# Another order for the steps of a planned attention-plus-MLP kernel

## The chip, the cores and the metric

The kernel runs on one core of one Trainium2 chip. The metric is the device time of one execution in microseconds, the median of several runs. Before the change it is 181.74 us (three runs, 180.81 to 182.94). The core's engines are PE (matmul), DVE (vector), ACT (scalar, activation), POOL (GpSimd) and SP, which issues nearly all of this kernel's DMAs from one queue. Each takes its instructions strictly in the order of its own list; semaphores tie the lists together.

## The reference

The first part is a linear attention with a decaying state, for batch 4, 8 heads, 768 steps and head size 48. Per head and step t:

```
cur   = (u * k_t) outer v_t
y_t   = r_t @ (state + cur)
state = w_t * state + k_t outer v_t
```

The second part is an MLP over the 3072 tokens (y with its heads laid side by side, 384 wide):

```
h = x @ w_in          # 384 -> 2048
g = max(0.01 * h, h)
out = g @ w_out       # 2048 -> 384
```

Inputs and output are float32.

## The kernel before, in words

**Tiling.** The sequence is cut into 24 chunks (named c0 to c23 here) of 128 steps, six for each of the four batches. The first two chunks of two batches are done as two *pairs* (c0 with c1, c2 with c3; the function `pair`), the other 20 one by one (`single`), some with their score matmuls merged. For a chunk, four DMAs load w, k, r and v (192 KB each) into one of ten `in` buffers. ACT takes the logarithm of w (L778, "Ln"), PE sums it over the steps with a triangular matrix (the *cum* step, L784 and L787), DVE makes an inclusive sum `ci` (L796), ACT takes exponents (L805, L810, L814), DVE multiplies them into r and k (L468), PE or a DMA transposes these (L479, L831), PE makes the scores (L925), DVE masks them (L855), and PE multiplies them with v (*intra*, L896) and the carried state with r (L891). PE also forms the chunk's contribution to the state (*sums*, L865, and L650 for a pair). POOL casts v to bf16 (`vb`, L518), scales the carried state (`sb`, L842), and makes the `u` term (*bonus*: L498 and L502 multiply, DVE reduces at L506, L510 gives `vs`). DVE adds the bonus (L541), and the output is transposed into `xT` (*typose*, L527, then a copy at L532 or L534, or a DMA at L910).

**The MLP** runs in 15 blocks (0 to 14) of one or two chunks. The *up* steps (L1087) multiply `xT` with `w_in`, ACT applies the leaky relu (L1102) into `g`, the *down* steps (L1117, four per chunk) multiply with `w_out`, ACT or DVE copies the result into one of five `o` buffers (L1128, L1130), and SP stores it (L1134). The last three blocks save matmuls with a seven-product scheme (`seven`: products L1019, sums L1002, combinations L1033, L1035, L1040, stores L1070). The weights are loaded in float32 at the start and cast to bf16 piece by piece on DVE, ACT or POOL (L411, L413, L415).

**What sets the order.** Every step above is added to a `Plan` as an entry with the engines that may do it and an assumed duration on each, a priority number, the steps it depends on, and the buffers it reads and takes. There are 1090 steps. Before any instruction is issued, `Plan.order` walks through assumed time: whenever an engine is free, it takes from the ready steps the one with the lowest priority number, if the buffers are there. The outcome is one list of steps per engine, and the steps are then issued in that order. Two tables are applied just before: `RANK` adds a number to the priority of single steps, and `FORCE` pins a step to one engine.

```
        for i, x in RANK.items():
            plan.steps[i][2] = round(plan.steps[i][2] + x, 3)
        for i, e in FORCE.items():
            plan.steps[i][0] = {e: plan.steps[i][0][e]}
        order = plan.order(pools)
```

In the first 24 us of assumed time, gaps on PE are filled with matmuls on zeros (L1159), as many as fit the assumed gap.

A *place* below is the position of a step in the list of its engine, from 0; an *entry* of SP is the same for its DMAs.

Of the kernel before, what the change touches and what calls it, by code (L numbers as in the profile page):

```python
# [23 lines left out]
class Plan:  # L24
# [135 lines left out]
STORE = (0.45, 8, 0.9, 0.2)  # L160
TRK = (1.7, 64, 0.9, -0.6)
TY = (0.95, 24, 0.7, -0.6)
RANK = {0: 15.37, 1: 14.4, 2: 3.33, 3: 23.03, 5: 38.76, 6: 12.01, 7: -26.8, 8: -21.87, 9: -21.96, 10: -19.05,
# [63 lines left out]
FORCE = {24: "DVE", 27: "DVE", 30: "ACT", 31: "DVE", 47: "ACT", 59: "ACT", 62: "ACT", 80: "ACT", 86: "DVE",  # L227
    113: "DVE", 115: "ACT", 118: "DVE", 120: "ACT", 122: "ACT", 124: "DVE", 126: "POOL", 128: "ACT", 129:
    "POOL", 135: "POOL", 138: "DVE", 140: "POOL", 143: "ACT", 144: "POOL", 493: "DVE", 501: "ACT", 605: "DVE",
    613: "ACT", 905: "DVE", 911: "DVE", 933: "ACT", 953: "ACT", 967: "ACT", 1003: "ACT", 1031: "ACT", 1076:  # L230
    "ACT", 1081: "ACT"}


@with_exitstack
def kernel(
# [95 lines left out]
    with tc.manual_schedule():  # L331
# [810 lines left out]
        step({"PE": 0.0}, lambda e: None, 1000.0, deps=[up_first[2]], reads=[warm])  # L1142
# [51 lines left out]
```

## Time and profile before

| | |
|---|---|
| median of three runs | 181.74 us (180.81 to 182.94) |
| the profiled execution, its own time | 180.97 us |
| its span, first to last instruction | 179.3 us |
| mean granted PE clock | 0.997 |
| PE busy | 170.3 us, 95% of the span |
| weight loads on PE | 133.8 us, 75% |
| DVE, ACT, POOL busy | 131.9, 116.5, 103.4 us |
| DMA: all transfers | 34.43 MB, mean 192 GB/s |
| `in` loads of a single chunk | 192 KB each, 4.2 us from issue to landing (median) |

Busy times are unions of an engine's instructions and are averages over stages with different limits: the first 24 us (loading, first pairs, weight casts), a long middle in which chunks and MLP blocks interleave, and the last 10 us, in which only the MLP's last products are left. Where an engine's row shows a wait, it names what ended last before the instruction could start. "issue" in the chain of waits is time in which nothing that the profile shows was waited for.

### The profile page before, as it was taken

The page shows a single profiled execution, that of the slowest core. Times are in us where ns is not written, and L with a number is a line of the kernel's source. Part 1 is how long each engine was busy: PE and PEld are TensorE (multiplying, and loading weights), DVE is VectorE, ACT ScalarE, POOL GpSimd, SP SyncE. Part 2 cuts the span into 40 slices and gives each one's busy share as a digit, 9 for nine tenths or more (in the row PEclk, how much of TensorE's full clock was granted, in tenths as well). Part 3 has the DMA queues.
Part 4 walks back from the last instruction along what each step waited for, and adds up shares of the span by engine and source line. Part 5 has one row for each costly group of instructions (what it writes and reads, how often), then busy time and mean ns, then how long its engine had stood idle before and what let it go on. Part 6 is the DMA issues. An engine that isn't in the chain of part 4 may idle for free.

```text
span 179.3 us, 5364 instructions
## 1 busy us (share of the span) xinstructions
PE 170.3 (95%) x2102; PEld 133.8 (75%) x2105; DVE 131.9 (74%) x266; ACT 116.5 (65%) x259; POOL 103.4 (58%) x138
## 2 busy tenths in 40 slices
PE   7798899999989999999999999999999999999991
PEld 2555778867868688787688777777778798899991
DVE  7799664189769899459687659499787599777472
ACT  4679868855957688895379775176685487735620
POOL 5998532675697586878468855414996448110000
PEclk9999999999999999999999999999999999999998
DMA  6999999999999899999999999979799996813004
GB/s 150 261 284 317 371 378 358 185 195 201 227 185 203 170 223 143 182 208 184 200 199 194 220 178 229 208 151 140 146 205 140 195 214 139 184 24 115 0 22 154
DMA packets 116716, 34.43 MB, mean 192 GB/s; under 512 B 109138, under 2 KB 115923, under 8 KB 116691
## 3 DMA queue, kind: packets, MB, share of 16 engines
q1 hardware_dynamic: 116688, 34.09, 94.6%
q8 instruction: 16, 0.26, 0.7%
q14 instruction: 10, 0.07, 0.2%
q10 hardware_dynamic: 2, 0.00, 0.0%
HBM read 25.17 MB, written 4.72 MB: 167 GB/s over the span
## 4 chain that ended last, share of the span: by engine, by line
PE 57%; DMA 12%; POOL 8%; issue 7%; SPq 6%; DVE 4%; ACT 4%; DVEq 0%; POOLq 0%; ACTq 0%
PE ps L1087 26%; PE ps L1117 14%; DMA in<-in_v_dram 8%; PE ps L1019 6%; SPq L553 4%; DMA in<-in_k_dram 3%; PE ps L925 2%; POOL ru L498 2%; SPq L389 2%; DMA in<-in_r_dram 2%; ACT g L1102 2%; POOL ru L502 2%; POOL sb L842 1%; DVE o L1040 1%; PE ps L896 1%
## 5 line engine op out<-in xcount | busy, mean ns | idle before, releaser
L1087 PE MATMUL ps<-xT,w_in_b 128*128 128x256 bf16 (+1 forms) x720 | 73.2, 251 | 0.2 <-ACT xT L534 0.2
L1102 ACT ACTIVATE g<-ps 128x512 bf16<-128x512 f32 x96 | 56.5, 595 | 20.7 <-PE ps L1087 15.2
L1087 PEld LDWEIGHTS <-w_in_b 128*128 128x128 bf16 x720 | 57.5, 98 | 9.2 <-issue 0.7
L1117 PE MATMUL ps<-w_out_b,g 128*128 128x384 bf16 x288 | 56.0, 326 | 0.1
L1117 PEld LDWEIGHTS <-g 128*128 128x128 bf16 x288 | 25.7, 97 | 12.3 <-ACT g L1102 0.2
L498 POOL TENSOR_TENSOR ru<-in,ub 128x384 f32<-128x384 f32 x24 | 24.6, 1028 | 11.0 <-DMA in<-in_k_dram 10.8
L468 DVE TENSOR_TENSOR rk<-in,ps 128x384 bf16<-128x384 f32 x48 | 25.0, 549 | 7.4 <-ACT ps L810 4.2
L855 DVE TENSOR_TENSOR m<-ps,maskb 128x512 bf16<-128x512 f32 x40 | 25.4, 684 | 6.1 <-PE ps L925 5.1
L502 POOL TENSOR_TENSOR ru<-ru,in 128x384 f32<-128x384 f32 x24 | 24.3, 1018 | 2.7 <-DMA in<-in_r_dram 2.1
L842 POOL TENSOR_TENSOR sb<-s,a 128x384 bf16<-128x384 f32 x18 | 15.7, 873 | 8.9 <-ACT a L805 8.7
L510 POOL TENSOR_TENSOR vs<-in,dg 128x384 f32<-128x384 f32 x20 | 16.6, 828 | 7.4 <-DVE dg L506 4.9
L518 POOL CAST vb<-in 128x384 bf16<-128x384 f32 x24 | 12.0, 504 | 12.0 <-DMA in<-in_v_dram 12.0
L506 DVE TENSOR_REDUCE dg<-ru 128x8 f32<-128x384 f32 x24 | 13.1, 546 | 2.3 <-POOL ru L502 2.1
L796 DVE TENSOR_TENSOR ci<-ps,lw 128x384 f32<-128x384 f32 x20 | 11.1, 554 | 3.7 <-PE ps L784 1.7
L778 ACT ACTIVATE lw<-in 128x384 bf16<-128x384 f32 x20 | 10.4, 520 | 3.0 <-DMA in<-in_w_dram 3.0
L810 ACT ACTIVATE ps<-ps 128x384 f32<-128x384 f32 x20 | 9.5, 474 | 4.1 <-DVE ci L796 3.8
L541 DVE TENSOR_TENSOR y<-ps,vs 128x384 bf16<-128x384 f32 x20 | 11.1, 554 | 1.4 <-PE ps L896 0.6
L880 DVE TENSOR_TENSOR s<-ps,sb 128x384 f32<-128x384 f32 x14 | 7.7, 552 | 3.9 <-PE ps L865 1.4
L814 ACT ACTIVATE ps<-ci 128x384 f32<-128x384 f32 x20 | 9.8, 488 | 0.6 <-DVE ci L796 0.6
L805 ACT ACTIVATE a<-ps 64x4 f32<-64x4 f32 x36 | 6.0, 167 | 5.6 <-DVE ci L796 3.8
L534 ACT COPY xT<-ps 128x384 bf16<-128x384 bf16 x11 | 5.2, 478 | 6.9 <-PE ps L527 6.9
L1019 PEld LDWEIGHTS <-g 128*128 128x128 bf16 x96 | 8.0, 98 | 0.5 <-ACT g L1102 0.4
(105 smaller groups left out, 222.3 us busy)
## 6 DMA issues: line engine op xcount, KB each, us to landing
out_dram<-o SPq DMA_DIRECT2D x23, 192.0 KB, 3.2
in<-in_w_dram SPq DMA_DIRECT2D x20, 192.0 KB, 4.2
in<-in_k_dram SPq DMA_DIRECT2D x20, 192.0 KB, 4.2
in<-in_r_dram SPq DMA_DIRECT2D x20, 192.0 KB, 4.3
in<-in_v_dram SPq DMA_DIRECT2D x20, 192.0 KB, 4.3
in<-in_moe_w_out_dram SPq DMA_DIRECT2D x4, 768.0 KB, 12.1
in<-in_moe_w_in_dram SPq DMA_DIRECT2D x4, 384.0 KB, 7.0
in<-in_moe_w_in_dram SPq DMA_DIRECT2D x2, 768.0 KB, 9.2
```

What stands on the lines that cost most here:

```text
L468: (nc.gpsimd if e == "POOL" else nc.vector).tensor_tensor(out=o, in0=x, in1=i, op=ALU.mult)
L498: lambda e: nc.gpsimd.tensor_tensor(out=ru.t[:], in0=kv(), in1=ubv, op=ALU.mult),
L502: lambda e: nc.gpsimd.tensor_tensor(out=ru.t[:], in0=ru.t[:], in1=rv(), op=ALU.mult),
L506: lambda e: nc.vector.tensor_reduce(out=dg.t[:], in_=ru.t[:], axis=AX.X, op=ALU.add),
L510: lambda e: nc.gpsimd.tensor_tensor(out=vs.t[:], in0=vv(), in1=dg.t[:].unsqueeze(2).to_broadcast([128, H, D]), op=ALU.mult),
L518: {"POOL": 0.56}, lambda e: nc.gpsimd.tensor_copy(out=vb.t[:], in_=vv()),
L842: lambda e: nc.gpsimd.tensor_tensor(out=sb.t[:].rearrange("p g a d -> p (g a) d"), in0=s_in.t[:].rearrange("p g a d -> p (g a) d"), in1=a_ ...
L855: lambda e, par=par: nc.vector.tensor_tensor(out=m.t[:, par, :, :], in0=sc[par].t[:].rearrange("p (g t) -> p g t", g=NP), in1=maskb[:].uns ...
L1019: nc.tensor.matmul(o(), lhsT=x()[:, i, :], rhs=y()[:, i, :], start=fresh, stop=(stop and i == ii[-1]), skip_group_check=True)
L1087: nc.tensor.matmul(hp.t[:, a * N : (a + 1) * N], lhsT=w_in_b[:, t, (j + a) * 128 : (j + a + 1) * 128], rhs=xT[:, t, c0 : c0 + N], start=(a ...
L1102: lambda e, hp=hp, g=g, j=j, J=J, N=N: nc.scalar.activation(out=g.t[:, j : j + J, 0:N], in_=hp.t[:, 0 : J * N].rearrange("p (a n) -> p a n ...
L1117: nc.tensor.matmul(op.t[:, 0:DM], lhsT=g.t[:, j, off : off + 128], rhs=w_out_b[:, j, :], start=(j == 0), stop=(j == NJ - 1))
```

## The change

Only the two tables `RANK` and `FORCE` are replaced. No step, no dependency, no buffer count and no assumed duration differs. In the kernel before, `RANK` has entries for steps 0 to 144, 492 to 716 and 902 to 1087, with gaps; in the changed one it has one for every step from 0 to 1087, and nearly all numbers differ. `FORCE` names 36 steps before and 55 after. By the words that come with the change, the numbers were searched with the operations lengthened at random and all results seen a little later than the plan assumes; neither is in the code, which plans with the same durations as before.

```diff
-RANK = {0: 15.37, 1: 14.4, 2: 3.33, 3: 23.03, 5: 38.76, 6: 12.01, 7: -26.8, 8: -21.87, 9: -21.96, 10: -19.05,
...
-    1083: 298.55, 1084: 18.56, 1085: 937.22, 1086: 932.94, 1087: 937.23}
-FORCE = {24: "DVE", 27: "DVE", 30: "ACT", 31: "DVE", 47: "ACT", 59: "ACT", 62: "ACT", 80: "ACT", 86: "DVE",
-    113: "DVE", 115: "ACT", 118: "DVE", 120: "ACT", 122: "ACT", 124: "DVE", 126: "POOL", 128: "ACT", 129:
...
+RANK = {0: 62.8, 1: 61.81, 2: -93.65, 3: -93.65, 4: 52.82, 5: 73.74, 6: -103.67, 7: -194.53, 8: -194.63, 9:
...
+    -18.67, 1083: 478.97, 1084: -18.68, 1085: 975.95, 1086: 975.96, 1087: 975.95}
+FORCE = {6: "DVE", 24: "DVE", 27: "ACT", 30: "ACT", 33: "DVE", 47: "ACT", 57: "ACT", 80: "DVE", 86: "ACT", 89:
+    "DVE", 103: "ACT", 113: "DVE", 115: "DVE", 120: "POOL", 128: "ACT", 129: "DVE", 132: "ACT", 134: "POOL",
...
```

What this does to the lists, counted in the two built programs:

| engine | steps before | steps after | at another place | mean shift, largest |
|---|---|---|---|---|
| PE | 320 | 320 | 245 | 2.7, 23 |
| DVE | 248 | 249 | 189 | 2.0, 19 |
| ACT | 258 | 260 | 198 | 2.6, 20 |
| POOL | 120 | 117 | 100 | 3.1, 11 |
| SP | 144 | 144 | 111 | 3.8, 37 |

41 steps change their engine, most of them copies and casts between DVE and ACT; POOL keeps one weight cast from before, takes two others, and gives five away. The moves that the prediction speaks of:

- SP: the w load of chunk 6 goes from entry 26 to 25, and c6's v load from 31 to 26; c5's v from 25 to 28; c7's k from 33 to 32. The stores of MLP blocks 0 (its first), 1 and 2 go from 27, 34 and 38 to 64, 60 and 65. The w loads of c9, c10 and c11 go from 43, 48 and 53 to 38, 42 and 44.
- PE: the cum steps of c5, c6, c9, c10 and c11 go from 67, 76, 111, 123 and 135 to 63, 72, 109, 121 and 131. The sums of c7 stay at 96. The last eight steps stay.
- POOL: c6's `vs` goes from behind c7's first bonus product to behind c7's cast of v.
- Weight casts: five go to DVE (four from POOL, one from ACT), two leave it (one to ACT, one to POOL); one goes from ACT to POOL and one from POOL to ACT.
- The line numbers of the changed kernel are 73 higher below the tables.

More of the change, by code (lines that the diff above doesn't have):

```diff
@@ L162 @@
 TY = (0.95, 24, 0.7, -0.6)
-RANK = {0: 15.37, 1: 14.4, 2: 3.33, 3: 23.03, 5: 38.76, 6: 12.01, 7: -26.8, 8: -21.87, 9: -21.96, 10: -19.05,
[63 rows of a table removed]
-FORCE = {24: "DVE", 27: "DVE", 30: "ACT", 31: "DVE", 47: "ACT", 59: "ACT", 62: "ACT", 80: "ACT", 86: "DVE",
-    113: "DVE", 115: "ACT", 118: "DVE", 120: "ACT", 122: "ACT", 124: "DVE", 126: "POOL", 128: "ACT", 129:
-    "POOL", 135: "POOL", 138: "DVE", 140: "POOL", 143: "ACT", 144: "POOL", 493: "DVE", 501: "ACT", 605: "DVE",
-    613: "ACT", 905: "DVE", 911: "DVE", 933: "ACT", 953: "ACT", 967: "ACT", 1003: "ACT", 1031: "ACT", 1076:
-    "ACT", 1081: "ACT"}
+RANK = {0: 62.8, 1: 61.81, 2: -93.65, 3: -93.65, 4: 52.82, 5: 73.74, 6: -103.67, 7: -194.53, 8: -194.63, 9:
[134 rows of a table added]
+FORCE = {6: "DVE", 24: "DVE", 27: "ACT", 30: "ACT", 33: "DVE", 47: "ACT", 57: "ACT", 80: "DVE", 86: "ACT", 89:
+    "DVE", 103: "ACT", 113: "DVE", 115: "DVE", 120: "POOL", 128: "ACT", 129: "DVE", 132: "ACT", 134: "POOL",
+    135: "DVE", 137: "ACT", 140: "DVE", 141: "DVE", 144: "POOL", 160: "ACT", 173: "ACT", 189: "ACT", 202:
+    "ACT", 238: "DVE", 262: "ACT", 311: "DVE", 341: "DVE", 343: "ACT", 384: "DVE", 420: "ACT", 422: "ACT",
+    436: "DVE", 501: "ACT", 613: "DVE", 737: "ACT", 743: "ACT", 757: "ACT", 771: "ACT", 785: "ACT", 821:
+    "ACT", 883: "ACT", 905: "ACT", 933: "DVE", 939: "ACT", 953: "ACT", 967: "ACT", 998: "ACT", 1003: "DVE",
+    1031: "ACT", 1076: "ACT", 1081: "ACT"}
 @with_exitstack
```

196 rows, old and new, of the table RANK are left out of this document.

## The prediction

> **What bounds the kernel now.** I read the page from the top first: the share of each engine, and the slices, which tell in which part of the span an engine is full.
>
> ```profile
> span 179.3 us, 5364 instructions
> ...
> PE   7798899999989999999999999999999999999991
> ...
> DMA  6999999999999899999999999979799996813004
> ```
>
> From the sixth slice on (22.4 us) PE is at nine tenths or more in all but the twelfth (49 to 54 us) and the last. DMA is full too, until about 155 us. The view of windows puts numbers to this; its columns are the stretch, its length, then busy time (and instructions) of PE, weight loads, DVE, ACT, POOL, then the granted clock, DMA share and GB/s.
>
> ```profile
> 24.00:48.00 24.00, 24.00 (x288) 18.78 (x286) 14.74 (x28) 17.45 (x36) 13.48 (x16) 1.00 1.12 249
> 48.00:72.00 24.00, 23.20 (x329) 18.77 (x327) 21.32 (x43) 18.15 (x44) 17.18 (x22) 1.00 1.05 189
> 72.00:168.00 96.00, 95.81 (x1106) 76.27 (x1104) 70.16 (x129) 61.67 (x142) 54.22 (x65) 1.00 0.95 170
> ```
>
> From 24 to 168 us PE is idle for 0.80 + 0.19 = 0.99 us of 144. Every matmul of the reference's work is in both kernels, so a new order can win only PE's waits. The view of waits names them; of PE's rows these matter:
>
> ```profile
> PE ps L865 <- POOL vb L518: 0.6, 1, 0.6
> ...
> PE ps L1019 <- DVE o L1040: 0.3, 1, 0.3
> ```
>
> The first is the wait of the twelfth slice, the second lies in the tail; PE's longer ones, in the head (before 24 us), come below. A shown wait is too short by a little, because an end on PE is modelled:
>
> ```profile
> 50.27 1.46 PE L1117 MATMUL ps<-w_out_b,g 128*128 128x384 bf16 x8
> 51.57 0.39 PE L479 MATMUL ps<-ident,rk 128*128 128x128 bf16 x4
> ```
>
> Eight matmuls started at 50.27 and the next form at 51.57, 1.30 us on, while their drawn end (51.73) is 0.16 later. So each wait is about 0.16 longer than shown, and one under 0.16 is not shown at all. Allowing for seven of them after 24 us, the tail's included: 0.99 + 0.3 + 7 x 0.16 = 2.4 us. That is the ceiling of what the order can win behind the head.
>
> **The change part by part.** Counted in the two built programs, of 320 PE steps 245 stand at another place (mean shift 2.7 places, most 23), of 144 SP entries 111 (mean 3.8, most 37); 41 steps go to another engine. Nothing is added but 6 fill matmuls (36 become 42), all in the head.
>
> *Head.* The chain of waits there:
>
> ```profile
> 11.47 8.26 DMA in<-in_v_dram
> ...
> 20.71 0.91 POOL vb L518 x2
> ...
> 21.66 0.47 PE ps L650 x13
> 22.13 0.02 issue
> 22.16 0.57 DVE sb L661
> ...
> 23.69 1.42 PE ps L1087 x12
> ```
>
> The v load of the second pair is entry 10 of SP in both lists (the first is 0), behind the same ten entries. POOL then has four steps for it: bonus, cast, cast, bonus before; cast, bonus, cast, bonus after. The second cast, which PE's state sums (L650) need, is third in both. PE's places 0 to 36 hold the same steps, and places 25 to 45 are the same up to one swap. The first gap-free run of L1087 therefore starts at 23.7 again. The fills added there are short and stand where PE waits anyway (three ahead of the add that needs DVE's sb). Head: 0, with 0.3 us either way as the bound.
>
> *Weight casts.* Five casts come to DVE from POOL and ACT, and two leave it. Their cover:
>
> ```profile
> 33.35 0.56 DVE L413 CAST w_out_b<-in 128x768 bf16<-128x768 f32 x1 [3.68 <-DMA in<-in_moe_w_out_dram]
> ```
>
> DVE is idle for 3.68 us until that weight lands. In the changed list it makes two casts behind that landing, to about 33.35 + 2 x 0.56 = 34.5, and PE's down step that needs them stands at place 58 in both lists, behind c4.cum at 57, which the chain of waits has at 35.36:
>
> ```profile
> 35.36 0.18 PE ps L784
> ```
>
> Cost 0; without that cover, 0.56 each.
>
> *The c6 load.* This is the one place where I find a new wait. PE's list goes there, in before:
>
> ```profile
> 41.13 0.36 PE L896 MATMUL ps<-vb,m 128*128 128x48 bf16 x8
> 41.33 1.46 PE L1117 MATMUL ps<-w_out_b,g 128*128 128x384 bf16 x8
> 42.63 0.33 PE L527 MATMUL ps<-ident,y 128*128 128x128 bf16 x3
> 42.80 0.81 PE L1117 MATMUL ps<-w_out_b,g 128*128 128x384 bf16 x4
> 43.45 0.39 PE L479 MATMUL ps<-ident,rk 128*128 128x128 bf16 x4
> 43.67 0.33 PE L784 MATMUL ps<-lw,trev 128*128 128x384 bf16 x1
> ```
>
> The last is c6.cum. It goes from place 76 to 72: the first row, half of the second, the third and fourth now stand behind it (0.20 + 0.65 + 0.17 + 0.65 = 1.67 us by starts; of the transposes one goes and one comes). PE would be there at 43.67 - 1.67 = 42.0. What it needs:
>
> ```profile
> 36.39 5.75 DMA in<-in_v_dram
> ...
> 42.65 0.52 ACT L778 ACTIVATE lw<-in 128x384 bf16<-128x384 f32 x1 [0.23 <-DMA in<-in_w_dram]
> ```
>
> ACT's Ln of c6 starts when its w has landed (42.6). In the changed list w stands one SP entry earlier, where c5's v was issued at 36.39 and landed at 42.14. With the Ln's 0.52 PE can start at about 42.7: a wait of 0.7. Loads pass SP about 1 us apart, so if w gains a whole entry it lands at 41.6 and the wait is 0.1. I take 0.5, nearer to the row of that very entry. What is queued behind c6.cum on PE (c4's intra, three downs) waits with it, and so do DVE's ci and ACT's exponents of c6.
>
> *The wait of L865.* It ends this piece of the chain:
>
> ```profile
> 44.28 5.07 DMA in<-in_k_dram
> ...
> 49.42 1.00 POOL ru L498
> 50.42 0.35 POOL vs L510
> ...
> 52.95 0.46 POOL vb L518
> ```
>
> The last row is c7's cast of v, and PE's sums of c7 (place 96 in both lists) wait for its end, 53.41. The change puts c6's vs (L510) behind that cast, 0.8 us by the starts around it, and takes two stores out of SP's way for one load more, so that k is issued one entry, about 1 us, earlier. The cast ends near 53.4 - 0.8 - 1.0 = 51.6; PE, late by the 0.5 above, comes at about 53.2. So the 0.6 + 0.16 goes. Late next is c6's vs itself, which PE needs for c6's transposes only 16 places on.
>
> *Tail.* The last eight PE steps and the last six of DVE keep their order. So its 0.3 stays; 0.3 either way as the bound.
>
> *The other places.* What the moves make of the stretch from 55 to 170 us I can't work out step by step from rows that show another order. Bounds: 1.3 us gained (2.4 less the L865 wait and the tail's 0.3 with its hidden part), 3.5 lost (rival B). I take 0, nearer to the waits that the windows show there (0.19 from 72 us on).
>
> Sum against the profiled execution: 180.97 (span 179.3, and 1.67 around it) + 0.5 - 0.76 = 180.7. That execution lies 0.77 below the median of the three runs shown, 181.74; the same step from the median gives **181.4** or 181.5; I give 181.4.
>
> **The rivals.** A measurement here tells about 1% (1.8 us) from no change.
>
> *A, all waits go:* the margins of the new order cover every wait. Time 181.74 - 2.4 = 179.3. For it: no wait of PE after 24 us is forced by the matmuls themselves. Against: DMA is as full as PE until 140 us, so not all loads can come earlier.
>
> *B, PE asks sooner than loads land (slower):* besides c6, the cum step of c5 goes from PE place 67 to 63, c9 from 111 to 109, c10 from 123 to 121, c11 from 135 to 131. Where w doesn't come as much sooner, PE stops at L784. Four places are some 1.7 us and two some 0.9; the margin by the c6 rows is 43.67 - 42.65 - 0.52 = 0.5. For five chunks, between 0.4 and 1.2 each, 0.7 on average: 3.5, so 185.2. It decides from where w lands less than about 0.6 us (Ln and hand-over) ahead of PE. Against: w of c9 to c11 moves 5, 6 and 9 SP entries ahead, at about 1 us each, and that of c5 two. Only c6 has clearly too little.
>
> *C, stores held back (slower):* the output stores of blocks 0, 1 and 2 go from SP places 27, 34 and 38 to 64, 60 and 65, and there are five o buffers.
>
> ```profile
> out_dram<-o SPq DMA_DIRECT2D x23, 192.0 KB, 3.2
> ```
>
> Block 5's second output copy finds a buffer only when the store of block 4 or 1 (places 58, 60) is through. If not, the copy waits, its PSUM bank stays taken, and PE's next downs wait. At most one store's 3.2 us; I take 2: 183.7.
>
> *D, PE isn't really full:* weight loads are busy for 113.8 us from 24 to 168, PE for 143.0. If the difference of 29 us were waits inside PE's busy time, an order could reach 181.7 - 29 = 153. Against it stands the row of eight 384-column matmuls in 1.30 us, one per 162 ns, none of which waits. The Trainium skill's page "Perfetto Trace Analysis", section "Identifying the Most-Contended Engine", calls matmul busy time a poor measure and points to the share of weight loads; by that rule a fifth would be open here, and the trace disagrees by that row.
>
> *E, nothing on the chip changes:* the waits only change places, 181.7.
>
> **How the numbers follow.** Forecast 0.52, A 0.13, B 0.21, C 0.09, D 0.02, E 0.03. Within 1% are the forecast and E, 0.55; faster A and D, 0.15; slower B and C, 0.30. The forecast's own range is 180.0 to 183.2: the bounds of head, c6 and tail, and part of the unshown stretch. The range given, 179.4 to 185.0, takes in C and half of B, and leaves out D, half of A and the upper half of B, about 0.2.
>
> **What would show it.** PE's L865 of c7 without a wait for vb. A wait at L784 near 42 us, for ACT's lw behind in_w. The first gap-free L1087 at 23.7, within 0.3. The last L1019 behind L1040, with about 0.3 again. PE's idle time from 24 to 168 between 0.4 and 1.5 us: under 0.3 is A; over 3 is B if the waits stand at L784, C if they stand at L1117 while copies of L1128 or L1130 wait (lines as in the kernel before). I am wrong if waits over 1 us turn up between 55 and 170 us for which no row of before speaks, or if the head ends more than 0.5 us off.

## The result and the profile after

The changed kernel takes 180.63 us, the kernel before 181.38 us (medians of 20 runs each, taken together); the ratio is 0.9949, with a 95% interval of 0.9927 to 0.997. The change makes the kernel faster by half a per cent. The forecast was 181.4 us from a median of 181.74 us.

The two profiled executions don't show this gain: that of the changed kernel took 181.48 us (span 179.8), that of the kernel before 180.97 us (span 179.3). The first lies 0.85 above its kernel's median, the second 0.41 below. So two traces laid side by side would mislead here, and most of what follows deals with that.

From the page of the changed kernel, the span and the slices:

```profile
span 179.8 us, 5386 instructions
...
PE   7899899999999999999999999999999999999991
...
DMA  5999999999999897999999999999999995722022
```

The twelfth slice of PE, which was not full before, is full now, and DMA is full until about 150 us, as it was. The view of windows of the changed kernel (stretch, length, then PE, weight loads, DVE, ACT, POOL with busy time and count, granted clock, DMA share, GB/s):

```profile
24.00:48.00 24.00, 23.65 (x278) 18.32 (x276) 13.65 (x27) 18.23 (x37) 10.82 (x13) 1.00 1.06 239
48.00:72.00 24.00, 23.46 (x331) 18.87 (x329) 19.86 (x41) 17.55 (x44) 16.13 (x20) 1.00 1.01 178
72.00:168.00 96.00, 95.50 (x1106) 75.93 (x1105) 72.23 (x135) 62.48 (x141) 57.16 (x68) 1.00 0.97 176
```

PE is idle for 0.35 + 0.54 + 0.50 = 1.39 us from 24 to 168 us, against 0.99 before: more, in an execution that is also slower. PE's timeline (start, length as drawn, line, tiles, count, and in brackets the idle time before it and what ended it) shows where. Lines are 73 higher than before.

```profile
23.44 1.48 PE L1160 MATMUL ps<-xT,w_in_b 128*128 128x256 bf16 x12
...
25.59 0.33 PE L600 MATMUL ps<-ident,y 128*128 128x128 bf16 x3
26.02 0.38 PE L1160 MATMUL ps<-xT,w_in_b 128*128 128x128 bf16 x4
...
41.86 0.39 PE L552 MATMUL ps<-ident,rk 128*128 128x128 bf16 x4
42.49 0.32 PE L857 MATMUL ps<-lw,trev 128*128 128x384 bf16 x1 [0.25 <-ACT lw L851]
...
53.15 0.39 PE L552 MATMUL ps<-ident,rk 128*128 128x128 bf16 x4
53.37 0.33 PE L938 MATMUL ps<-vb,rk 128*128 128x96 bf16 x4
...
71.13 0.40 PE L552 MATMUL ps<-ident,rk 128*128 128x128 bf16 x4 [0.43 <-DVE rk L541]
...
128.69 0.83 PE L1160 MATMUL ps<-xT,w_in_b 128*128 128x128 bf16 x12 [0.29 <-DMA xT<-y]
...
175.56 0.82 PE L1092 MATMUL ps<-w_out_b,in 128*128 128x192 bf16 x8 [0.31 <-DVE o L1113]
```

The up matmuls begin at 23.44 (23.62 before). Three transposes at 25.59 need 0.17 us, but the next matmul starts 0.43 later, at 26.02: 0.26 of waiting, of which nothing is marked. At 42.49 stands c6's cum behind ACT's Ln (0.25 shown, 0.41 by the starts). The sums of c7 (L938) follow the transposes without a gap. New are waits at 71 and 128 us, and shorter ones, unmarked in the view, at 52, 88, 90 and 94 us.

Since drawn ends hide part of a wait, I counted *late starts* in each trace: how much later a matmul starts than its predecessor's usual step allows, every case over 0.13 us, from the first gap-free up run to the end. The experiments below divide these into places that show in every execution, those with the wide loads of a later section included ("fixed"), and the rest. In us:

| profiled execution | its own time | up run starts | late starts | fixed | rest |
|---|---|---|---|---|---|
| before | 180.97 | 23.62 | 2.27 | 1.50 | 0.77 |
| before, again | 182.06 | 23.64 | 3.68 | 1.50 | 2.18 |
| changed | 181.48 | 23.44 | 3.16 | 0.74 | 2.42 |
| changed, again | 182.33 | 23.54 | 3.75 | 0.74 | 3.01 |
| before, wide loads | 179.81 | 23.49 | 1.50 | 1.50 | 0 |
| changed, wide loads | 179.14 | 23.44 | 0.73 | 0.73 | 0 |

The fixed places before are at 62 us (0.37), 132 us (0.17 and 0.22), 149 us (0.26) and the tail (0.48); in the changed kernel 25.7 us (0.26) and the tail (0.47). The difference is 0.76 us, as large as the gain in the medians (0.75). The up run also starts 0.05 to 0.18 us earlier in the changed kernel, which this count leaves out.

### The profile page after: what moved, and what is told of

It reads as the page before. It is cut to its first block, busy times and chain, and to the rows that moved or that the text cites. A ratio compares the mean times of both kernels' runs of the same rounds, so it can differ in the third digit from the quotient of the medians.

```text
span 179.8 us, 5386 instructions
## 1 busy us (share of the span) xinstructions
PE 171.2 (95%) x2111; PEld 134.2 (75%) x2111; DVE 131.1 (73%) x267; ACT 117.9 (66%) x261; POOL 101.8 (57%) x135
## 4 chain that ended last, share of the span: by engine, by line
PE 54%; DMA 21%; POOL 8%; SPq 6%; issue 4%; ACT 3%; DVE 2%; POOLq 0%; DVEq 0%; ACTq 0%
PE ps L1160 24%; PE ps L1190 15%; PE ps L1092 7%; DMA in<-in_k_dram 6%; DMA in<-in_w_dram 5%; DMA in<-in_r_dram 5%; SPq L841 4%; POOL ru L575 3%; DMA xT<-y 3%; DMA in<-in_v_dram 2%; PE ps L998 2%; POOL ru L571 1%; PE ps L857 1%; POOL vb L591 1%; POOL y L583 1%
## 5 line engine op out<-in xcount | busy, mean ns | idle before, releaser
L1190 PEld LDWEIGHTS <-g 128*128 128x128 bf16 x288 | 25.6, 97 | 12.6
L591 POOL CAST vb<-in 128x384 bf16<-128x384 f32 x24 | 13.1, 553 | 11.4 <-DMA in<-in_v_dram 11.4
L915 POOL TENSOR_TENSOR sb<-s,a 128x384 bf16<-128x384 f32 x18 | 14.9, 829 | 7.8 <-ACT a L878 7.7
L1203 ACT COPY o<-ps 128x384 f32<-128x384 f32 x14 | 6.7, 478 | 6.2 <-PE ps L1190 3.7
L1232 PE MATMUL ps<-zeros 128*128 128x128 bf16 (+1 forms) x42 | 8.6, 327 | 1.3 <-DVE zeros L405 1.3
L552 PE MATMUL ps<-ident,rk 128*128 128x128 bf16 x88 | 8.3, 219 | 1.0 <-DVE rk L541 0.9
```

The lines of the kernel that those rows point to most:

```text
L591: {"POOL": 0.56}, lambda e: nc.gpsimd.tensor_copy(out=vb.t[:], in_=vv()),
L915: lambda e: nc.gpsimd.tensor_tensor(out=sb.t[:].rearrange("p g a d -> p (g a) d"), in0=s_in.t[:].rearrange("p g a d -> p (g a) d"), in1=a_ ...
L1190: nc.tensor.matmul(op.t[:, 0:DM], lhsT=g.t[:, j, off : off + 128], rhs=w_out_b[:, j, :], start=(j == 0), stop=(j == NJ - 1))
```

## The experiments

### Both kernels a second time

No edit. Three theories: M (margins), that the new order loses less where loads land late; F (fixed places), that some waits which stand in every execution are gone; H, that it is the head.

> The changed kernel, unaltered, a second time. Theory M (margins): the gain of about 0.5% is a mean over executions; which PE wait appears changes from execution to execution, so the ratio comes out at 0.993 to 0.997 again, while this profile shows other waits after 24 us than the last one, at least two of the 0.25 to 0.6 us ones gone or moved. Rival F (fixed places): the gain is the same few waits each time; then the waits at 42, 52, 71 and 128 us stand again at the same places with the same lengths within 0.1 us. Rival H (head): the first gap-free run of up matmuls starts again 0.2 us before that of the kernel before.

> The kernel before, unaltered, timed against itself: ratio 1.000 within 0.003, which is the size of a difference that says nothing. Theory M: its profile shows waits at other places than the last one, and its PE idle time from 24 to 168 us is above the 0.99 us of the last profile, near 1.5 to 2, since that profile came from an execution 0.4 below the median. Rival F: the L865 wait of 0.6 at 52.6 us stands again and the idle time is 0.99 within 0.2.

Measured: the changed kernel again 180.68 us against 181.82, ratio 0.9952 (0.9923 to 0.998); the kernel before against itself 1.0006 (0.9981 to 1.0031). So the half per cent is there a second time, and a kernel against itself shows nothing of the kind. PE's timeline of the changed kernel, second execution:

```profile
42.66 0.32 PE L857 MATMUL ps<-lw,trev 128*128 128x384 bf16 x1 [0.26 <-ACT lw L851]
...
95.29 0.32 PE L857 MATMUL ps<-lw,trev 128*128 128x384 bf16 x1 [1.03 <-ACT lw L851]
```

and of the kernel before, second execution:

```profile
52.95 0.33 PE L865 MATMUL ps<-vb,rk 128*128 128x96 bf16 x4
53.85 0.32 PE L784 MATMUL ps<-lw,trev 128*128 128x384 bf16 x1 [0.56 <-ACT lw L778]
...
62.79 0.92 PE L1087 MATMUL ps<-xT,w_in_b 128*128 128x256 bf16 x7 [0.20 <-ACT xT L534]
...
90.22 1.47 PE L1087 MATMUL ps<-xT,w_in_b 128*128 128x256 bf16 x12 [0.71 <-DMA xT<-y]
```

Both theories are partly right. In the changed kernel the waits at 42, 52 and 71 us stand again (0.42, 0.36 and 0.51 us by the starts, 0.41, 0.28 and 0.59 in the first execution), while those at 94 and 107 us grew or are new, and the one at 128 us is gone. In the kernel before, the wait at 62 us is the same to 0.01 us, but the L865 wait on which the prediction rested is not there: the next step waits for another load at the same place (0.73 by the starts). PE's idle time from 24 to 168 us is 1.89 us in that execution, as M had it. A wait for a load can stand in two executions or move about; the five fixed places of before, which the later runs show to need no load, stand in both. Which of the two kinds makes the gain, these traces can't tell.

### The order of the DMAs alone, and the order of the engines alone

The lists that the planner makes are written out, and an engine takes only the next entry of its list:

```diff
-                    want, ok = {}, True
+                    want, ok = {}, LISTS[e][at[e]] == i
```

SP's list is then that of the other kernel.

> The kernel before, with only SP's list (all loads, stores and transposing DMAs) in the changed kernel's order; PE, DVE, ACT and POOL keep theirs. Theory L (loads): the gain is that loads of w come earlier and stores stand back, ratio 0.994 to 0.997. Theory M (the orders fit each other): nothing of the gain or a loss, 0.999 to 1.010, with waits of PE for work that hangs on loads which now come later (c5's v, c7's k).

> The changed kernel with SP's list in the order of before; the four engines keep the changed order. Theory L: the gain goes, ratio 1.000 or above, and where the cum steps come earlier on PE than w lands (c6 at 42 us, c9 to c11 later) PE waits at L-lines of cum for lw, 0.5 to 1.2 us each, so 1.005 to 1.02 as rival B of the prediction had it. Theory M without loads (engine order alone carries the gain): 0.995.

Measured: 215.12 us, ratio 1.1808 (1.1757 to 1.1859), and 215.24 us, 1.1864 (1.1825 to 1.1903). All theories missed this by far. The waits of PE in the first of the two (us in total, times, longest), and a window of it:

```profile
PE ps L923 <- POOL vb L576: 22.4, 6, 10.6
```

```profile
72.00:96.00 24.00, 13.14 (x115) 9.56 (x115) 6.50 (x13) 9.27 (x22) 9.87 (x14) 0.82 0.67 134
```

Six waits for POOL's cast of v (L576, line 518 before) make 22.4 us. The chain of waits around the first of the long ones reads:

```profile
72.27 3.95 DMA in<-in_v_dram
...
76.27 0.51 POOL vb L576
```

This load is c10's v. It stands at entry 51 of SP's list before and at 57 of the changed one. SP's timelines of the kernel before and of the changed kernel have it at

```profile
62.95 1.01 SPq L768 DMA_DIRECT2D in<-in_v_dram  x1
```

```profile
72.01 0.94 SPq L841 DMA_DIRECT2D in<-in_v_dram  x1
```

SP has it at 72.27 here, so it is hardly behind the changed kernel's times; the changed list just asks for this v 9 us later than the list of before, and PE, in the order of before, stands for 4.85 us. From then on SP's entries wait in turn for engines that stand still with PE: its transposing DMAs of DVE's products (L889) wait 14.0 us in six waits, up to 5.9 at once, where the kernel before has 3.0 in three. In the second run PE's waits are spread over more steps, 12.7 us of them for casts of v. Each list is good only with the other; neither half of the change is a part that can be had alone.

### Shorter loads

To take the loads out, the chunk loads of c4 to c23 move the same bytes from rows that lie together: pieces of 1536 bytes in place of 192. The values land elsewhere, so what is computed is not the reference's; every instruction and every order stays.

```diff
-nc.sync.dma_start(out=part(i)(), in_=src[b, :, t0 : t0 + L, :].rearrange("h p d -> p h d"))
+rows_of = src[b].rearrange("h s d -> (h s d)")[t0 * DM : (t0 + L) * DM]
+nc.sync.dma_start(out=part(i)(), in_=rows_of.rearrange("(p h d) -> p h d", p=L, h=H))
```

> The kernel before, with the chunk loads of c4 to c23 taking the same number of bytes from rows that lie together (1536 bytes a piece in place of 192), so the values land in other places; the order stays. This makes the loads shorter and leaves every other step. Theory M (the changed order wins where loads land late): the waits for lw, vb and for transposing DMAs that came and went between executions vanish, time 179.5 to 181, and the scatter shrinks. Rival F (the gain is in fixed waits, not in loads): 181 to 182 as before.

> The same for the changed kernel. Theory M: its gain over the kernel before with the same loads shrinks from 0.9 us to under 0.3 us, or turns round. Rival F and rival H (the head's 0.15 us and the fixed waits): 0.9 us stay between the two.

Measured: 179.87 us for the order before (all runs from 179.81 to 180.01; ratio 0.9944, 0.9924 to 0.9963) and 179.13 us for the changed order (178.86 to 179.19; 0.9897, 0.987 to 0.9924), against the same runs of the kernel before, 180.82 us. The runs of a kernel, which ranged over some 2 us with the loads as they were, now agree to 0.2 and 0.33 us. That is what M said of the loads, and F, with 181 to 182, had not. But the difference between the orders stays, at 0.74 us, where M had under 0.3: the gain is not tolerance to late loads. With the loads as they were both kernels lose the same to them: 1 - 0.9944 and 0.9952 - 0.9897, both about 0.55%, 1.0 us.

With the loads out, one trace of each shows the rest plainly. PE, kernel before with wide loads (one line is added, so L1088 is L1087):

```profile
60.57 0.82 PE L1118 MATMUL ps<-w_out_b,g 128*128 128x384 bf16 x4
61.59 1.58 PE L1088 MATMUL ps<-xT,w_in_b 128*128 128x256 bf16 x13 [0.20 <-ACT xT L534]
...
130.18 0.83 PE L1088 MATMUL ps<-xT,w_in_b 128*128 128x128 bf16 x12
131.02 0.32 PE L785 MATMUL ps<-lw,trev 128*128 128x384 bf16 x1
131.18 0.24 PE L788 MATMUL ps<-ones,lw 128*128 128x1 bf16 x4
131.50 0.82 PE L1118 MATMUL ps<-w_out_b,g 128*128 128x384 bf16 x4
...
147.92 1.75 PE L1020 MATMUL ps<-w_out_b,g 128*128 128x192 bf16 x16
```

Four down matmuls take 0.65 us; at 60.57 the next starts 1.02 later, so 0.37 are lost, for a copy to `xT` on ACT. At 131.02 and 131.50 the same reckoning gives 0.17 (for a Ln) and 0.22 (for a `g`). The sixteen at 147.92 are drawn 1.75 us long, against 1.48 for such a row without a stop in the changed kernel: inside them lie the 0.26 of the place at 149 us, for the last `g`. None of these needs a load. ACT comes late because of the order of its own list, as the single moves below show for the first three. ACT around the first of them:

```profile
60.69 0.35 ACT L806 ACTIVATE a<-ps 64x4 f32<-64x4 f32 x2 [1.08 <-DVE ci L797]
61.06 0.48 ACT L534 COPY xT<-ps 128x384 bf16<-128x384 bf16 x1
```

The copy, whose transposes PE had done by 60.0, stands behind two small exponents of c9, and those wait 1.08 us for DVE's `ci`. In the changed kernel, with the same wide loads, the two exponents stand ahead of that copy too, but c9's cum comes two places earlier on PE: it starts 0.91 us ahead of the copy's transposes, against 0.27 before. `ci` is there sooner, and ACT waits for the transposes instead:

```profile
59.63 0.35 ACT L879 ACTIVATE a<-ps 64x4 f32<-64x4 f32 x2
60.23 0.48 ACT L607 COPY xT<-ps 128x384 bf16<-128x384 bf16 x1 [0.25 <-PE ps L600]
```

### More loads

The opposite: behind each w and each v load of c4 to c23 one more DMA of 24 KB into a tile that nothing reads.

```diff
+                    if i in (0, 3):
+                        nc.sync.dma_start(
+                            out=junk[(2 * n + i // 3) % 3][:], in_=src[b, 0:1, t0 : t0 + L, :].rearrange("h p d -> p h d"))
```

> The kernel before, with a further DMA of 24 KB into an unused tile behind every w load and every v load of c4 to c23 (40 more in SP's list). Theory M: loads land later and the time rises by over 1.5 us, since PE's places hang on loads with little to spare. Rival F: the loads have time to spare, the time rises by under 0.5 us.

> The same for the changed kernel. Theory M: it loses less than the kernel before does, the difference between the two grows from 0.9 to over 1.5 us. Rival F: the difference stays at 0.9 within 0.5. If the changed order asks for w sooner without having loads to spare (rival B of the prediction), it loses more than the kernel before, with waits for lw.

Measured: 189.88 us for the order before, ratio 1.0475 (1.0431 to 1.0519), and 194.86 us for the changed one, 1.0727 (1.0672 to 1.0782). Loads have next to nothing to spare in either kernel, and the changed order loses more (14.9 us over its usual ratio of 0.995, against 9.1 us), the reverse of M. The waits of PE before:

```profile
PE ps L1091 <- DMA xT<-y: 4.0, 3, 1.6
PE ps L788 <- ACT lw L782: 2.0, 3, 0.7
```

and in the changed kernel:

```profile
PE ps L1164 <- DMA xT<-y: 6.2, 3, 2.4
PE ps L553 <- DVE rk L542: 2.8, 5, 1.4
```

Where it loses more it does so for transposing DMAs in the same queue and for products of k or r, and not for `lw`, which rival B had named. One reserve: the three tiles are used in turn, and SP waits for one of them to be free 8.0 us in the changed kernel and 3.9 us before, as w and v loads stand closer together there. Part of the larger loss is the experiment's own, so how much the changed order itself loses more is not shown.

### Single moves, with the wide loads

If four fixed waits are the gain, moving just the steps that cause them should give it without the rest of the change. In the lists of before, in words:

```diff
 ACT: ... c8's evac, 
+         c7's copy to xT,
          c9's two exponents a,
-         c7's copy to xT, ...
 ACT: ... M11's g,
+         c20's Ln,
          c21's exponents, 
-         c20's Ln, ...
 PE:  ... down of block 11,
+         block 12: product with a stored difference,
          block 12: plain products,
-         block 12: product with a stored difference, ...
```

> The kernel before with the loads of 1536-byte pieces and three moves of one step: c7's copy to xT (the one that PE waits for at 61 us) ahead of c9's two small exponents on ACT, c20's Ln ahead of c21's exponents on ACT (131 us), and on PE block 12's product with a stored difference (place 281) ahead of its plain products (place 280, which wait for the last g at 148 us). All other steps keep the order of before. Theory F (the gain is four fixed waits, 0.37 + 0.17 + 0.22 + 0.26 us, gone, less 0.26 for a new one at 25.7 us): these four go and nothing else changes, 179.87 - 1.02 = 178.85, within 0.15, which is below the changed kernel's 179.13 with the same loads. If the gain is something else (a rival R: the rest of the 245 moved places): 179.6 to 179.9.

Measured: 179.01 us (178.82 to 179.34; ratio 0.9893, 0.9871 to 0.9915), 0.86 us below the order before with the same loads; theory F had 178.70 to 179.00. Two moves did what was expected, the third nothing. ACT and then PE at the first place:

```profile
60.42 0.48 ACT L592 COPY xT<-ps 128x384 bf16<-128x384 bf16 x1 [0.56 <-PE ps L585]
60.94 0.35 ACT L864 ACTIVATE a<-ps 64x4 f32<-64x4 f32 x2
```

```profile
60.82 0.82 PE L1176 MATMUL ps<-w_out_b,g 128*128 128x384 bf16 x4
61.48 1.69 PE L1146 MATMUL ps<-xT,w_in_b 128*128 128x256 bf16 x14
...
147.42 1.10 PE L1078 MATMUL ps<-in,g 128*128 128x192 bf16 x8
148.35 1.32 PE L1078 MATMUL ps<-w_out_b,g 128*128 128x192 bf16 x14
```

The down steps take their 0.66 us and the up run follows at once. At 147.42 eight matmuls of 0.082 take 0.93: the wait of 0.27 stands as before, now in the product that was moved ahead, which needs the last `g` as well. The late starts fell from 1.50 to 0.74 us, which is the two moves' 0.37 + 0.17 + 0.22. (The traced execution, 179.34 us, shows 0.47 of this in its time, as its up run started at 23.74, 0.25 later than in the kernel before with the same loads.) So two steps, each moved by a few places on ACT, give with these loads what the whole change gives (179.01 and 179.13 us). Why the wait at 149 us is gone in the changed kernel is not shown.

The other way round, the head: up to 26.5 us of the plan the lists of the kernel before, from there the changed ones.

> The changed kernel with the loads of 1536-byte pieces, and for all steps that the kernel before starts in the first 26.5 us of its plan the lists of the kernel before, engines included; from there on the changed lists. Theory F: the wait at 25.7 us for DVE's copy to xT goes (0.26), the first gap-free run of up matmuls starts 0.05 later, 179.13 - 0.21 = 178.9, within 0.15. Rival H (the changed head carries part of the gain): 179.2 to 179.9.

Measured: 178.58 us (178.49 to 178.77; ratio 0.9872, 0.9851 to 0.9894), 0.55 below the changed kernel with the same loads, more than the 0.2 expected.

```profile
25.72 0.33 PE L658 MATMUL ps<-ident,y 128*128 128x128 bf16 x3
25.89 1.28 PE L1219 MATMUL ps<-xT,w_in_b 128*128 128x128 bf16 x20
```

The wait at 25.7 us is gone, and only the tail's 0.47 is left of late starts. By PE's last start the two traces differ by 0.16 us (173.54 and 173.70), by their own times by 0.65 (178.49 and 179.14); the 0.49 between lies behind the last matmul and around the span, and I can't name its cause. Rival H falls: the changed head costs a little.

### The same two with the loads as they were

> The kernel of the last run with the loads as they were (192-byte pieces): lists of before up to 26.5 us of the plan, the changed lists from there. Theory F: the waits for loads cost here what they cost in both kernels, about 1 us over the wide loads, with scatter; so 0.2 to 0.5 us below the changed kernel, ratio to before 0.990 to 0.994, and the profile has no wait at 25.7 us. If the changed head is what makes later loads land in time: 0.997 or above.

> The kernel before with the loads as they were and the same three single moves (two on ACT's list, one on PE's). With wide loads the two on ACT took their 0.76 us and the one on PE nothing. Theory F: the same here, ratio to before 0.996 (0.993 to 0.999), as large as what the whole change gives; the profile has no wait at 62 and 132 us and one at 149 us. Rival R: no gain, 0.999 to 1.002, because waits for loads turn up in their place.

Measured: the mixed kernel (head of before, rest changed) 180.35 us against 182.13, ratio 0.9917 (0.988 to 0.9954), and no wait at 25.7 us in its trace, both as expected. It beats the kernel before, and by its ratio also the changed one (0.9949 and 0.9952), though the intervals overlap. The three moves: 181.89 us, ratio 0.9975 (0.994 to 1.001). This is within what was expected and doesn't settle it: the trace has no late start at 62 and 132 us, but 2.7 us of waits for loads, among them these, the second at a step that had none before:

```profile
53.67 0.32 PE L842 MATMUL ps<-lw,trev 128*128 128x384 bf16 x1 [0.41 <-ACT lw L836]
...
71.62 0.32 PE L842 MATMUL ps<-lw,trev 128*128 128x384 bf16 x1 [0.61 <-ACT lw L836]
```

The first of the two stands ahead of the moves; behind them it may be that a step made 0.37 us earlier comes 0.37 us earlier to the next load too, which is not shown. Whether the moves give their 0.76 us under the real loads, a mean over some ten runs with a scatter of 2.5 us can't say.

## Why the prediction was right or wrong

**The time** lay 0.8 us below the forecast of 181.4 (its sum, carried out, is 181.48), inside its range and within 1% of before. Of the 0.8, 0.36 is the kernel before, whose median came to 181.38 in 20 runs; against the same runs the change gained 0.75 us where the sum had 0.26. That the sum was on the right side of zero is luck: its one gain, the wait of L865, hangs on a load, and loads cost both kernels the same.

**The ceiling** of 2.4 us of late starts was right for that execution (2.27), and so was taking each wait as longer than shown. The Trainium skill's page "Perfetto Trace Analysis", section "Tensor Engine Instruction (MATMUL, LD_WEIGHTS)", says that an end on this engine is estimated and not observed; the starts agree with it, 0.41 against 0.25 shown at 42.49. What the ceiling lacked was that only 1.50 of the 2.27 come in every execution.

**Head:** 0, with 0.3 either way, held: the up run starts 0.05 to 0.18 earlier. But the step "the same places on PE, so the same head" missed a 0.26 wait right behind it, at 25.7 us for DVE's copy to `xT`, on which the changed kernel's DVE timeline has

```profile
25.61 0.36 DVE L605 COPY xT<-ps 128x384 bf16<-128x384 bf16 x1 [1.16 <-ACT g L1175]
```

Before, that copy is made at 25.38. PE's list was the same there; DVE's and ACT's were not. Why it waits for that `g` was not taken apart further; the lists of before don't have it.

**Weight casts:** 0 was right; no late start stands between 26.1 and 41 us.

**The c6 load:** place, cause and size were right (0.41 and 0.42 for 0.5). It vanishes with the wide loads, so it is a load that lands late, as was argued.

**The wait of L865:** it is gone, as forecast, but counting it as 0.76 gained was wrong. It is a load's wait, and in the second execution of before it was not there either; another stood in its place. All waits for loads together cost about 1.0 us in both kernels.

**Tail:** 0.31 shown for 0.3, right.

**The other places** from 55 to 170 us, taken as 0, are the step that failed. Four fixed waits stood there, 1.02 us in all. One was in the view of waits (0.2 for ACT's `xT` copy), the others are too short to be shown; I argued from the idle time of 0.19 in the windows, which hides 0.16 of each. With them the sum is 0.26 - 1.02 = -0.76 from the fixed places and, on average, nothing from the loads: 181.38 - 0.76 = 180.62, and 180.63 was measured. That this agrees to 0.01 is luck too, as the interval of the ratio is 0.8 us wide. With the wide loads the runs show it directly (0.74 us); with the loads as they were it rests on both kernels losing about 1.0 us to loads, and the three single moves didn't confirm it there.

**The rivals.** A: not all waits went. B: PE does ask sooner than w lands, at 42, 94 and 107 us, but that is balanced by other loads' waits; with more loads the changed order did lose more, but not at `lw`. Of the signs named in advance, all held in the first trace (no wait at L865, 42.49 behind `lw`, 23.44, the tail's 0.31, 1.39 us idle), and still the gain lay elsewhere: none of them looked at the places that made it. The sign of being wrong, a wait over 1 us between 55 and 170, turned up in the second execution (1.03 at 95.29). C: no wait at a down step stood behind a copy. D: in the mixed kernel with wide loads the window from 24 to 168 us reads

```profile
24.00:168.00 144.00, 144.00 (x1740) 115.86 (x1739) 107.77 (x206) 99.89 (x225) 82.95 (x100) 1.00 0.65 187
```

PE is busy for all of 144 us and weight loads for 115.86, and by starts no wait over 0.13 us is left in it. In this stretch the time that weight loads leave open is not there to be won. E: not so; waits did go.

## What to carry to other kernels

When a difference is half a per cent and executions of one kernel differ by one, a pair of traces can have the wrong sign. Take away what varies, here with loads in longer pieces, and compare then: the runs of one kernel then agreed to between 0.2 and 0.5 us, and both the gain and its places could be read from one trace each. In a kernel whose main engine is full, sum short waits by starts and ask of each whether it needs a load; those that only need another engine's list in another order are the ones that the new order won here. And the list of a DMA queue and the lists of the engines are one thing: either alone, taken from another good order, cost 18 and 19%.

## What the runs showed of the hardware that I had not expected

Pieces of 1536 bytes in place of 192 lowered the DMA share at the same rate. Before, and with wide loads, from 24 to 168 us:

```profile
24.00:168.00 144.00, 143.01 (x1717) 113.82 (x1715) 106.22 (x199) 97.27 (x221) 84.88 (x102) 1.00 1.00 186
```

```profile
24.00:168.00 144.00, 143.61 (x1727) 114.73 (x1726) 106.74 (x202) 98.27 (x223) 85.12 (x102) 1.00 0.69 187
```

186 and 187 GB/s, at shares of 1.00 and 0.69. A full DMA row was short pieces, not bytes (the longer pieces also lie together in memory, which these runs don't separate). The Trainium skill's page "DMA: Bandwidth & Descriptors", section "Specifications", puts the smallest transfer for full rate at 512 bytes, which agrees with that.

The stops of PE in the kernel with the foreign SP list also cost clock. From 72 to 96 us, where PE was busy for 13.14 of 24 us, the granted clock was 0.82; in the kernel before it was 1.00 there. Behind a stop of 4.85 us it was 0.53 from 77 to 80 us:

```profile
76.83 0.33 PE L923 MATMUL ps<-vb,rk 128*128 128x96 bf16 x4 [4.85 <-POOL vb L576]
```

Behind a stop of 3.46 us that ended at 120.04 it was 1.00 (120 to 126 us). The Trainium skill's page "TensorE: Matmul & The Clock Gate", section "Part 1: The HAM clock gate (the "warmup" mystery)", has the clock fall after an idle window of about 3.4 us. The longer stop agrees with that; the shorter one, hardly above it, brought no lower clock.
